# A gated mix of attention and GLU on one core: first key weights in pieces, x turned in four parts, one load moved, all work in a new order

## The chip, the core and the metric

The kernel runs on one core of a Trainium2 chip. The core has a matrix engine (TensorE, PE in the profile), a vector engine (DVE), an engine for activations (ACT), a general one (POOL) and one that only issues DMAs (SP). Each runs its own instructions in order; semaphores connect them. The metric is the device time of one execution in microseconds (us), the median of several runs.

## What is computed

x is 2048 tokens by 512. Two branches read it, and a sigmoid of x·gate_w mixes them per token. Branch A is attention with 32 heads of 16, in 4 segments of 512 tokens, with a memory M, z carried from one segment to the next. Branch B is a gated linear unit of inner width 1792. All weights are bfloat16.

```python
for s in range(N):                       # N = 4 segments of L = 512 tokens
    logits = einsum('bhqd,bhkd->bhqk', qs, ks) * scale + mask
    a_dot = einsum('bhqk,bhkd->bhqd', softmax(logits), vs)
    pq = phi(qs)                         # phi(t) = t+1 if t>0 else exp(t)
    a_mem = einsum('bhld,bhde->bhle', pq, M) / (einsum('bhld,bhd->bhl', pq, z)[..., None] + 1e-06)
    outs.append(g * a_mem + (1.0 - g) * a_dot)
    M = M + einsum('bhld,bhle->bhde', phi(ks), vs);  z = z + phi(ks).sum(over l)
a = concat(outs) @ wo
b = (gelu(x @ w_gate) * (x @ w_up)) @ w_down
return gate * a + (1 - gate) * b         # gate = sigmoid((x * gate_w).sum(-1))
```

## The kernel before

The program is a list of tasks. A task is a few instructions on one engine, or on one of two (an eviction of a PSUM bank can go to ACT or to DVE). `dense` makes a group of four products of 512 columns into one of four PSUM banks. For segment s the groups are K{s}_{t}, Q{s}_{t} (t = 0 to 3), G{s}_{ft} (gate) and U{s}_{ft} (up), ft = 0 to 13, all at L448; V{s}_{m}a and b are half groups of 256 and 257 columns (L498), where column 257 gives the token gate. `Kev`, `Qev`, `Vev`, `Gev` are their evictions, `gd` and `gelu` the activations of the gate, `h` the product of gate and up, `out` the down product (L734), `wo` the output product (L748), `wev` and `oev` their evictions, `dma` the stores. Attention: `st{s}_{t}{A..E}` fills all of the scores' buffer psX (L601), `exp` takes it through the exponential to one of ten buffers (ACT, L608), `msk` masks it (POOL, L614), `pv` multiplies with V (L643), two head groups at a time. Then `tp`, `pvp`, `ota`, `otm` (DVE) bring it to the output's layout. Memory: `phk`, `phq` (a, b, c) compute phi, `ktr` and `otr` are DMA transposes, `mz` the memory's update (L576), `nd` and `ndp` its reading (L546). `vsh` copies V to a second layout by DMA.

The order of all tasks is written out by hand, as one long string `ORDER`: each word is a task, `:d` or `:a` chooses DVE or ACT, `:2` chooses bank 2. The order among the tasks of one engine is that engine's program; the dependencies are turned into semaphore waits. So any wait of an early task holds everything behind it on its engine, SP's DMA issues too.

The start. x of segment 0 arrives in two ways: tokens 0 to 255 as two plain loads of 128 KB (x0_0 on SP, x0_1 on ACT, issued at L341 like all plain loads) that PE turns with eight 128-column transposes (`xtr0_p`, L785; `xev0_p`, L794, copies them), and tokens 256 to 511 by two DMA transposes (x0_t2, x0_t3, L361). wk comes in halves of 256 KB, blocks 2 and 3 on SP and blocks 0 and 1 on ACT. The first key products K0 are cut in parts: a (blocks 2, 3) and b (blocks 0, 1) for tokens 0 to 255, c (all blocks) for the other tokens, 256 columns each (L476), 32 products in all. Before and between, PE runs 52 small products of ones (`warm1`, `warm2`, L382) that nothing reads. Further loads, all on SP in the order of `ORDER`: wq in halves, gate_w (gw), beta (to all 128 partitions), wv, the gate weights wg0, the four transposes of x of segment 1 (x1_0 to x1_3, L345), the up weights wu1, and later wg1, wd0, wd1, wu0, wo and x2. wv waits for x0_t3, wg0 for wq1, x1 for wq0, wu1 for wg0, x2 for wu1, wo for wu0.

Of the kernel before, what the change touches and what calls it, by code (L numbers as in the profile page):

```python
# [248 lines left out]
def _build(es, nc, A_x, A_wq, A_wk, A_wv, A_wo, A_beta, B_w_gate, B_w_up, B_w_down, gate_w, out):  # L249
# [131 lines left out]
    for name, n, cols in (("warm1", 45, 80), ("warm2", 7, 80)):  # L381
        one(name, PE, 3.0, [I(lambda e, cols=cols: e.matmul(BK[s0.i][:, 0:cols], ones, ones[:, 0:cols], start=True, stop=True),  # L382
                              [], [bk(s0)]) for _ in range(n)], bias=9000.0, opens=name == "warm1")
# [400 lines left out]
    for p in (1, 0):  # L784
        one(f"xtr0_{p}", PE, 4 * T_TR, [I(lambda e, q=q, kb=kb, p=p: e.transpose(  # L785
            XB[:, 1024 * p + (kb % 2) * 256 + q * 128:1024 * p + (kb % 2) * 256 + q * 128 + 128],
            pt[stage[0]][:, q, kb * 128:(kb + 1) * 128], ident[:, :]),
            [("xs", 0, 0), ("xs", 0, 1), ("pt", stage[0]), ("ident",)], [("X", p)]) for kb in (2 * p, 2 * p + 1) for q in (0, 1)])
# [79 lines left out]
Qev0_2:d phka0_0 V1_2b:1 V0_0a:3 G1_6:2 V1_0b:0 Vev1_2b:d phka0_2 st0_0E Vev0_0a:d Vev1_0b:d G0_1:1 bexp Gev1_6:a  # L868
exp0_0E Gev0_1:d Q1_2:3 V1_3b:2 V1_3a:0 kpada0_3 Qev1_2:d Vev1_3a:d phkb0_2 phkc0_2 Vev1_3b:d st0_1A gz0 gqa exp0_1A
gr0 Q1_0:1 V1_0a:3 G1_5:0 Vev1_0a:d gqb Gev1_5:d st0_1B Q1_1:2 K1_0:3 exp0_1B phkb0_0 ld_wu1 ld_x2_0 G0_5:0 Qev1_0:d  # L870
kpadb0_3 vsh0_21 st0_1C exp0_1C Qev1_1:d ld_x2_1 ld_x2_3 ktr0_3 ld_wg1 Gev0_5:d V1_2a:1 K1_3:2 K1_1:0 vsh0_01
Vev1_2a:a vsh0_20 ld_x2_2 ktr0_2 vsh0_00 ld_wd1 st0_1D phkc0_0 Kev1_1:d kpada1_1 G0_4:1 G0_3:0 Gev0_4:d Kev1_0:d
Gev0_3:d Kev1_3:a ld_wd0 ld_wu0 ktr0_1 ktr0_0 vsh1_20 ld_wo V1_1a:2 Vev1_1a:d exp0_1D st0_2A exp0_2A msk0_0B msk0_0D
msk0_0C kpada1_0 msk0_0E goa0 gob0 msk0_0A msk0_1A msk0_1C msk0_1D gfull msk0_1B G0_0:1 Q1_3:3 G1_1:0 Qev1_3:d phqa1_0
st0_2B Gev0_0:d Gev1_1:a pv0_1:2301 exp0_2B tp0_d01 tp0_d00 pvp0_01 Q2_0:3 Qev2_0:d tp0_d11 st0_2C K1_2:2 Kev1_2:d
pvp0_00 tp0_d10 gelu0 G0_8:3 G0_13:1 gd0_13 G0_10:2 G0_11:0 G0_9:1 gd0_8 gd0_10 gd0_9 gd0_11 G0_12:3 G0_7:2 gd0_12
G1_2:1 U0_0:0 gd0_7 Gev1_2:d pvp0_11 h0_0 U0_13:3 U0_10:2 h0_10 Q2_1:1 Qev2_1:d exp0_2C st0_2D mz0:0 U0_7:2 U0_9:1
pvp0_10 h0_13 exp0_2D phqb1_0 st0_2E exp0_2E phka1_0 h0_7 mza0 h0_9 ota0_0 phqa1_2 kpadb1_0 G1_4:3 U0_1:2 h0_1
Gev1_4:a V1_1b:0 st0_3A G1_0:1 U0_5:3 Q2_2:2 exp0_3A Vev1_1b:a Gev1_0:a Qev2_2:a kpadb1_1 st0_3B exp0_3B U0_11:0
U0_4:1 U0_12:2 st0_3C phkb1_0 exp0_3C phqc1_0 kpada1_2 h0_4 h0_5 U0_6:1 U0_2:3 h0_11 h0_12 phqb1_2 h0_2 G1_3:0  # L880
Gev1_3:d h0_6 kpadb1_2 st0_3D phka1_2 U0_3:2 h0_3 U0_8:3 h0_8 Q2_3:0 Qev2_3:d exp0_3D phkb1_2 msk0_2A msk0_2B msk0_2C
msk0_3A msk0_2E msk0_2D msk0_3C goc0 msk0_3B st1_0A msk0_3D pv0_3:1230 exp1_0A st1_0B exp1_0B tp0_d20 tp0_d21 pvp0_20
tp0_d30 ota0_1 pvp0_21 tp0_d31 kpada1_3 out0_1_0:1 out0_1_1 out0_1_2 V2_0a:2 Vev2_0a:d G1_9:3 V2_1b:0 Vev2_1b:d
wev0_1:d st1_0C G1_8:2 G1_10:0 G1_11:1 gelu1 gd1_9 G1_7:3 gd1_8 gd1_10 gd1_7 gd1_11 G1_13:2 gd1_13 G1_12:0 gd1_12
phqc1_2 phkc1_0 mzq0 pvp0_31 pvp0_30 ota0_3 V2_0b:3 Vev2_0b:d ota0_2 V2_1a:1 Vev2_1a:d out0_0_0:2 out0_0_1 out0_0_2
nd1_0:0 ndp1_0 phkc1_2 exp1_0C st1_0D exp1_0D K2_0:3 K2_2:1 wev0_0:d Kev2_0:d Kev2_2:a K2_1:0 st1_0E Kev2_1:d U1_2:2
h1_2 wo0_1:1 nd1_3:3 nd1_1:0 exp1_0E st1_1A ld_x3_2 vsh1_00 vsh2_01 ktr1_1 ktr1_0 oev0_1 ndp1_1 wo0_0:2 oev0_0
kpada2_0 vsh1_21 out0_2_0:1 nd1_2:0 msk1_0C msk1_0A exp1_1A st1_1B exp1_1B msk1_0B gz1 msk1_0E msk1_1A msk1_0D msk1_1B
out0_2_1 wo0_2:2 ndp1_2 st1_1C exp1_1C nd1_5:0 out0_2_2 ndp1_3 wev0_2:a ndp1_5 out0_3_0:3 st1_1D nd1_4:0 out0_3_1
out0_3_2 ktr1_2 dma0 vsh1_01 otr1_3 ndp1_4 otr1_0 oev0_2 phka2_0 msk1_1C wev0_3:d ktr1_3 dma1 vsh2_00 otr1_1 ld_x3_1  # L890
ld_x3_0 ld_x3_3 exp1_1D st1_2A exp1_2A gr1 msk1_1D pv1_1:1023 st1_2B exp1_2B tp1_d01 tp1_d00 kpadb1_3 V2_2b:0
Vev2_2b:d K2_3:1 Kev2_3:a G2_3:0 pvp1_00 Gev2_3:d tp1_d10 st1_2C U1_8:1 G2_1:0 otr1_2 V2_3a:2 h1_8 Gev2_1:d Vev2_3a:d
kpadb2_0 kpadb2_1 exp1_2C st1_2D phkb2_0 exp1_2D G2_6:1 wo0_3:0 U1_3:2 pvp1_01 tp1_d11 Gev2_6:a h1_3 phka2_2 oev0_3
st1_2E U1_0:3 V2_3b:1 G2_0:2 Gev2_0:d h1_0 Vev2_3b:d exp1_2E phkb2_2 st1_3A mz1:0 G2_4:2 G2_5:3 pvp1_10 mza1 Gev2_5:d
exp1_3A st1_3B exp1_3B Gev2_4:d U1_11:1 G2_2:0 Gev2_2:d ota1_0 U1_13:3 h1_13 U1_10:2 h1_10 h1_11 G2_11:0 G2_10:3
pvp1_11 phkc2_0 phkc2_2 ota1_1 otm1_0 otm1_1 G2_12:2 G2_9:1 st1_3C gelu2 gd2_11 gd2_12 G2_7:0 G2_13:2 gd2_10 gd2_9
gd2_7 gd2_13 G2_8:3 gd2_8 U1_7:1 U2_9:0 K3_0:2 h1_7 U2_5:3 Q3_0:1 phqa2_0 h2_9 h2_5 Qev3_0:d Kev3_0:d exp1_3C st1_3D
exp1_3D U1_1:0 U2_12:3 msk1_3A msk1_2A msk1_3B U2_13:1 h2_12 h1_1 h2_13 kpada2_1 st2_0A U1_9:2 V2_2a:3 U2_7:0 msk1_2D
msk1_2B msk1_2E h1_9 Vev2_2a:d vsh2_20 dma2 dma3 ktr2_0 ktr2_2 vsh2_21 exp2_0A phqb2_0 msk1_3D msk1_2C msk1_3C st2_0B
h2_7 kpada2_2 pv1_3:1230 tp1_d21 exp2_0B tp1_d20 V3_1a:2 Vev3_1a:a st2_0C exp2_0C pvp1_21 tp1_d31 U1_6:1 Q3_1:2  # L900
V3_0a:0 st2_0D h1_6 pvp1_20 Vev3_0a:d Qev3_1:a V3_2b:1 U1_4:2 U1_5:0 exp2_0D st2_0E exp2_0E tp1_d30 phqc2_0 h1_5 h1_4
ota1_2 Vev3_2b:a U1_12:3 h1_12 pvp1_31 pvp1_30 out1_1_0:0 st2_1A V3_1b:2 out1_1_1 V3_3a:3 exp2_1A st2_1B msk2_0B
msk2_0D Vev3_3a:a exp2_1B out1_1_2 U2_4:1 msk2_0E goa1 gob1 kpadb2_3 kpada2_3 msk2_0C msk2_0A msk2_1A ota1_3 h2_4
otm1_2 otm1_3 K3_1:3 mzq1 Vev3_1b:a wev1_1:a st2_1C msk2_1B goc1 U2_1:2 Q3_3:1 V3_0b:0 Kev3_1:d kpada3_0 h2_1 Qev3_3:d
kpadb2_2 exp2_1C msk2_1C st2_1D V3_2a:3 U2_6:2 exp2_1D Vev3_2a:a wo1_1:1 Vev3_0b:d kpadb3_0 h2_6 oev1_1 st2_2A msk2_1D
pv2_1:0231 exp2_2A st2_2B exp2_2B tp2_d00 pvp2_00 phqa2_2 tp2_d01 tp2_d10 pvp2_10 pvp2_01 tp2_d11 out1_0_0:0 out1_0_1
# [52 lines left out]
```

## Time and profile before

| | us |
|---|---|
| median of three runs | 263.89 |
| the runs | 263.14, 263.89, 518.72 |
| the profiled execution | 264.53 |
| its span, first to last instruction of the program | 262.8 |

The span is what the profile's page and the trace's views show; times in them are from its start. A row of the page's groups, for example, reads: line, engine, operation, what is written and read with shapes, count, then busy time, mean length of one, and the engine's idle time before them:

```
L608 ACT ACTIVATE pt<-psX 128x2048 bf16<-128x2048 f32 x72 | 135.1, 1877 | 29.5 <-PE psX L601 27.9
L614 POOL TENSOR_TENSOR pt<-pt,ctri 128x256 bf16<-128x256 bf16 x128 | 92.6, 734 | 128.3 <-ACT pt L608 123.8
L448 PE MATMUL psD<-xT,wu 128*128 128x512 bf16 x224 | 54.6, 380 | 0.0
L448 PE MATMUL psD<-xT,wg 128*128 128x512 bf16 x224 | 53.4, 380 | 1.1 <-DMA wg<-in_B_w_gate_dram 1.1
```

Matrix products are pipelined: one of 512 columns is 380 ns long, but the next starts 216 ns after it. The distance from start to start is what counts for PE's time. In the same execution 15.68 MB went over SP's DMA queue and 0.39 MB over ACT's.

### The profile page before, as it was taken

The numbers are of one execution on the slowest core, as the hardware profiler recorded it, in microseconds if no ns is written. First come the engines' busy times: TensorE is split into PE (matmuls) and PEld (weight loads), VectorE is DVE, ScalarE is ACT, GpSimd is POOL, SyncE is SP. The second block draws the span as 40 slices with busy tenths as digits, with TensorE's granted clock in tenths as the row PEclk, the third lists the DMA queues.
The fourth block names the chain that finished last, engine by engine and source line by source line (L and its number), as shares of the span: only waits on it lengthen the run. The fifth ranks groups of instructions, "written<-read, shape, count | busy, mean of one in ns | idle before, by whom it ended". The sixth has DMA issues, their size and how long they took to land.

```text
span 262.8 us, 6704 instructions
## 1 busy us (share of the span) xinstructions
PE 257.9 (98%) x2849; PEld 122.5 (47%) x2849; DVE 197.4 (75%) x412; ACT 203.2 (77%) x171; POOL 99.1 (38%) x163
## 2 busy tenths in 40 slices
PE   8989999999999999999999999999999999999995
PEld 8645445444454444544445445444444434444542
DVE  1658878284888686778968988976895973899873
ACT  1569879889998878898988898788788788777312
POOL 5006672024500465104806284156500477345300
PEclk9999999999999999999999999999999999999999
DMA  7795699300010211430003100022430000001432
GB/s 186 244 160 144 163 278 275 93 2 1 5 28 2 61 43 39 91 75 2 2 0 71 35 0 2 2 41 61 68 79 0 2 1 22 3 0 42 62 42 80
DMA packets 31974, 16.50 MB, mean 63 GB/s; under 512 B 21576, under 2 KB 31944, under 8 KB 31944
## 3 DMA queue, kind: packets, MB, share of 16 engines
q1 hardware_dynamic: 31528, 15.68, 27.2%
q8 instruction: 22, 0.36, 0.6%
q10 hardware_dynamic: 416, 0.39, 0.4%
q14 instruction: 8, 0.07, 0.1%
HBM read 7.87 MB, written 2.10 MB: 38 GB/s over the span
## 4 chain that ended last, share of the span: by engine, by line
PE 92%; DMA 4%; SPq 1%; issue 0%; DVE 0%; DVEq 0%
PE psD L448 47%; PE psD L734 19%; PE psX L601 9%; PE psD L643 6%; PE psD L748 5%; PE psD L498 5%; DMA wg<-in_B_w_gate_dram 3%; PE psD L546 1%; DMA wq<-in_A_wq_dram 1%; SPq L361 1%; PE psD L576 1%; SPq L341 1%; DVE ost L752 0%; DVEq L817 0%
## 5 line engine op out<-in xcount | busy, mean ns | idle before, releaser
L608 ACT ACTIVATE pt<-psX 128x2048 bf16<-128x2048 f32 x72 | 135.1, 1877 | 29.5 <-PE psX L601 27.9
L614 POOL TENSOR_TENSOR pt<-pt,ctri 128x256 bf16<-128x256 bf16 x128 | 92.6, 734 | 128.3 <-ACT pt L608 123.8
L448 PE MATMUL psD<-xT,wu 128*128 128x512 bf16 x224 | 54.6, 380 | 0.0
L448 PE MATMUL psD<-xT,wg 128*128 128x512 bf16 x224 | 53.4, 380 | 1.1 <-DMA wg<-in_B_w_gate_dram 1.1
L734 PE MATMUL psD<-wd,gb 128*128 128x512 bf16 x224 | 53.2, 380 | 0.0
L719 DVE TENSOR_TENSOR gb<-psD,gb 128x512 bf16<-128x512 f32 x56 | 37.2, 681 | 10.8 <-PE psD L448 10.7
L448 PEld LDWEIGHTS psD<-xT,wg 128*128 128x128 bf16 x224 | 20.8, 98 | 25.8 <-issue 2.6
L734 PEld LDWEIGHTS psD<-wd,gb 128*128 128x128 bf16 x224 | 20.7, 98 | 24.3 <-issue 2.1
L448 PEld LDWEIGHTS psD<-xT,wu 128*128 128x128 bf16 x224 | 20.2, 98 | 24.7 <-issue 2.6
L601 PE MATMUL psX<-qT,kD 32*128 32x192 bf16 (+7 forms) x512 | 28.5, 287 | 0.0
L529 DVE STREAM_TRANSPOSE tT<-psD 128x512 f32<-128x512 f32 x32 | 21.7, 701 | 5.6 <-PE psD L643 5.1
L442 DVE CAST gb<-psD 128x512 bf16<-128x512 f32 x20 | 13.6, 689 | 13.7 <-PE psD L448 13.7
L601 PEld LDWEIGHTS psX<-qT,kD 32*128 32x128 bf16 x512 | 8.2, 92 | 25.1 <-ACT pt L608 13.4
L498 PE MATMUL psD<-wv,xT 128*128 128x257 bf16 (+1 forms) x128 | 18.2, 273 | 0.0
L752 DVE SCALAR_TENSOR_TENSOR ost<-psD,gtok,wds 128x512 bf16<-128x512 f32 (+1 forms) x17 | 11.9, 711 | 7.7 <-PE psD L748 7.6
L667 DVE SCALAR_TENSOR_TENSOR ob<-tT,gq,rc 128x256 bf16<-128x256 f32 x32 | 16.7, 522 | 1.1
L702 ACT ACTIVATE gb<-psD 128x512 bf16<-128x512 f32 x28 | 15.0, 594 | 3.3 <-PE psD L448 3.3
L643 PE MATMUL psD<-pt,vnat 64*17 64x192 bf16 (+7 forms) x512 | 17.1, 283 | 0.0
L643 PE MATMUL psD<-pt,vsh 64*17 64x192 bf16 (+7 forms) x512 | 17.1, 283 | 0.0
L448 PE MATMUL psD<-xT,wq 128*128 128x512 bf16 x64 | 16.3, 379 | 0.0
L748 PE MATMUL psD<-wo,oT 128*128 128x512 bf16 (+1 forms) x68 | 16.2, 367 | 0.0
L498 PEld LDWEIGHTS psD<-wv,xT 128*128 128x128 bf16 x128 | 11.8, 97 | 6.6 <-issue 1.4
(81 smaller groups left out, 257.0 us busy)
## 6 DMA issues: line engine op xcount, KB each, us to landing
out_dram<-ost SPq DMA_DIRECT2D x15, 128.0 KB, 1.8
wg<-in_B_w_gate_dram SPq DMA_DIRECT2D x2, 896.0 KB, 6.5
wu<-in_B_w_up_dram SPq DMA_DIRECT2D x2, 896.0 KB, 8.3
wd<-in_B_w_down_dram SPq DMA_DIRECT2D x2, 896.0 KB, 7.1
vsh<-vnat SPq DMA_DIRECT2D x16, 68.0 KB, 2.9
wq<-in_A_wq_dram SPq DMA_DIRECT2D x2, 256.0 KB, 3.5
...
```

The costliest lines, as they stand in the source:

```text
L448: one(name, PE, n * T_MM, [I(lambda e, i=i: e.matmul(BK[sl.i][:, :], lhs(i), rhs(i), start=(i == 0), stop=(i == n - 1)), reads(i), [bk(sl) ...
L498: one(f"V{s}_{m}{'ab'[hf]}", PE, 2 * T_MM, [I(lambda e, i=i, sl=sl, a=a, z=z, xs=xs: e.matmul(BK[sl.i][:, 0:z - a], xs(i), wv[:, i, a:z], ...
L529: one(f"tp{name}", DVE, 0.605, [I(lambda e, sl=sl, ti=ti: e.transpose(tT[ti][:, :], BK[sl.i][:, :]), [bk(sl)], [("tT", ti)])], bias=bias)
L601: ins.append(I(lambda e, t=t, kb=kb, ncol=ncol, c0=c0, g=g: e.matmul(XALL[:, g * 512 + c0:g * 512 + c0 + ncol], kD[(4 * s + t) % R_KD][32 ...
L608: one(f"exp{s}_{name}", ACT, 2048 * 0.000833 + 0.05, [I(lambda e: e.activation(pt[slot][:, :, :], xin, ACTF.Exp, scale=ATT_SCALE), [("X",) ...
L614: ins.append(I(lambda e, mv=mv: e.tensor_tensor(mv, mv, cm, ALU.mult), [("pt", slot), ("causal",)], [("pt", slot)]))
L643: ins.append(I(lambda e, kb=kb, slot=slot, c0=c0, n=n, g=g, r0=r0, sl=banks[j], va=va: e.matmul(BK[sl.i][32 * g:32 * g + 17, 64 * kb:512], ...
L667: I(lambda e, ti=ti, ri=ri, t=t, j=j, dst=dst: e.scalar_tensor_tensor(out=dst, in0=t_rows(ti), scalar=gq[:, 2 * t + j:2 * t + j + 1], in1= ...
L702: t = one(f"gd{s}_{ft}", ACT, 0.485, [I(lambda e, gi=gi, f=f, sl=sl: e.activation(gb[gi][:, f, :], BK[sl.i][:, :], ACTF.Gelu_apprx_tanh), ...
L719: one(f"h{s}_{ft}", DVE, 0.605, [I(lambda e, sl=sl, gi=gi, f=f: e.tensor_tensor(gb[gi][:, f, :], BK[sl.i][:, :], gb[gi][:, f, :], ALU.mult ...
L734: mm.append(I(lambda e, fb=fb, gi=gi, f=f, q=q, sl=sl: e.matmul(BK[sl.i][:, :], gb[gi][:, f, q], wd[:, fb, :], start=(fb == 0), stop=(fb = ...
L748: one(f"wo{s}_{qt}{sfx}", PE, 4 * T_MM * w / 512, [I(lambda e, kb=kb, q=q, so=so, c=c, w=w: e.matmul(BK[so.i][:, 0:w], oT[:, kb, q], wo[:, ...
```

## The change

1. wk is loaded in three pieces: block 2 on SP (128 KB), block 3 and then blocks 0 and 1 on ACT.
2. The PE transposes of x and their copies are cut in four parts of 256 columns, one for each block, in the order 2, 3, 0, 1, each to its own bank of psX; blocks 2 and 3 are copied by DVE, 0 and 1 by ACT.
3. The warm-up products are 52 of 66 columns in one task ahead of the transposes, instead of 45 and 7 of 80 around them.
4. `ORDER` is new as a whole. At the start: the load of beta stands behind the four transposes of x1; identity on POOL stands behind `masks` and `causal0`; each K0 part c follows its part b earlier; Q0_0 stands ahead of the last eight key products; the first gate product (G0_5 now, G0_6 before) stands behind three Q groups and seven V halves; V products of segment 1 follow soon after. SP's order behind x1 is now beta, vsh0_20, wu1, x2_0, vsh0_01, vsh0_00, wg1, ktr0_0, wd1, vsh0_21, ktr0_1, vsh1_00, x2_1, x2_2, wu0, ktr0_2, ktr0_3, x2_3, wd0, wo. The tasks, their number and their instructions are otherwise the same.

```diff
-    for eng, h in ((SP, 1), (ACT, 0)):
-        ld_w(f"wk{h}", eng, wk[:, halves[h], :], wsrc(A_wk)[:, halves[h], :], [("wk", 2 * h), ("wk", 2 * h + 1)], 0.25)
+    for eng, nm, c in ((SP, "2", slice(2, 3)), (ACT, "3", slice(3, 4)), (ACT, "0", slice(0, 2))):
+        ld_w(f"wk{nm}", eng, wk[:, c, :], wsrc(A_wk)[:, c, :], [("wk", i) for i in range(c.start, c.stop)], 0.125)
...
-    for name, n, cols in (("warm1", 45, 80), ("warm2", 7, 80)):
-        one(name, PE, 3.0, [I(lambda e, cols=cols: e.matmul(BK[s0.i][:, 0:cols], ones, ones[:, 0:cols], start=True, stop=True),
-                              [], [bk(s0)]) for _ in range(n)], bias=9000.0, opens=name == "warm1")
+    one("warm1", PE, 3.0, [I(lambda e: e.matmul(BK[s0.i][:, 0:66], ones, ones[:, 0:66], start=True, stop=True),
+                             [], [bk(s0)]) for _ in range(52)], bias=9000.0, opens=True)
...
-    for p in (1, 0):
-        one(f"xtr0_{p}", PE, 4 * T_TR, [I(lambda e, q=q, kb=kb, p=p: e.transpose(
-            XB[:, 1024 * p + (kb % 2) * 256 + q * 128:1024 * p + (kb % 2) * 256 + q * 128 + 128],
+    for kb in (2, 3, 0, 1):
+        one(f"xtr0_{kb}", PE, 2 * T_TR, [I(lambda e, q=q, kb=kb: e.transpose(
+            XB[:, 1024 * kb + q * 128:1024 * kb + q * 128 + 128],
             pt[stage[0]][:, q, kb * 128:(kb + 1) * 128], ident[:, :]),
...
+        dst, xin, wr = xT[0][:, kb, 0:256], XB[:, 1024 * kb:1024 * kb + 256], [("xT", 0, kb, "h0")]
...
 ORDER = """
-ld_x0_0 ld_wk1 ld_x0_1 warm1:0 ident xtr0_1 xev0_1:d xtr0_0 warm2 xev0_0:d vones0 masks ld_wk0 causal1 gwz ld_x0_t2
-ld_x0_t3 ld_wq0 ld_wq1 ld_gw ld_beta causal0 consts K0_1a:1 K0_3a:2 K0_3b K0_2a:3 K0_0a:0 K0_2b K0_0b K0_1b K0_0c
-K0_2c K0_3c K0_1c Kev0_0:d Kev0_2:d kpadb0_0 kpadb0_2 causal kpada0_0 Kev0_3:a Q0_0:0 Qev0_0:a Q0_1:3 st0_0A gwtr:2
-Kev0_1:d gwev Q0_3:0 ld_wv ld_wg0 Qev0_1:d V0_1b:1 V0_3a:2 V0_3b:3 exp0_0A Qev0_3:d Vev0_3a:a Vev0_1b:a st0_0B
-Vev0_3b:d kpada0_2 kpada0_1 V0_0b:0 V0_1a:2 V0_2a:1 Vev0_0b:d G0_6:3 Gev0_6:d Vev0_1a:d Vev0_2a:d exp0_0B st0_0C
-exp0_0C Q0_2:0 G0_2:3 V0_2b:2 ld_x1_2 ld_x1_1 betab ld_x1_3 ld_x1_0 st0_0D Vev0_2b:a exp0_0D Gev0_2:d kpadb0_1
...
+ld_x0_0 ld_wk2 ld_x0_t2 masks ld_x0_1 ld_wk3 ld_wk0 causal0 vones0 ld_x0_t3 ld_wq0 ld_wq1 gwz ld_gw ident warm1:0
+xtr0_2 xtr0_3 xtr0_0 xtr0_1 xev0_2:d xev0_0:a xev0_1:a xev0_3:d K0_0a:1 K0_2a:2 K0_1a:3 K0_3a:0 K0_1b K0_1c K0_0b
+K0_0c Kev0_1:d K0_2b K0_3b Kev0_0:a kpada0_0 kpadb0_0 ld_wv Q0_0:3 ld_wg0 Qev0_0:a K0_3c gwtr:1 K0_2c ld_x1_0 Kev0_2:d
+kpadb0_2 ld_x1_1 ld_x1_2 st0_0A Q0_3:3 Q0_2:2 Kev0_3:a phka0_0 gwev kpada0_1 Qev0_2:d Qev0_3:d V0_2a:0 exp0_0A st0_0B
+ld_x1_3 V0_3b:1 V0_3a:2 Vev0_3b:d Vev0_2a:a V0_2b:0 consts V0_1b:3 V0_0a:1 exp0_0B st0_0C Vev0_3a:a Vev0_0a:d
+Vev0_2b:d V0_0b:2 Vev0_0b:d kpadb0_1 kpada0_3 G0_5:1 V0_1a:0 Vev0_1a:d phkb0_0 Q0_1:2 exp0_0C st0_0D Qev0_1:d
+Vev0_1b:d Gev0_5:a V1_3a:0 V1_1a:1 Vev1_1a:d V1_0a:2 Q1_2:3 exp0_0D Vev1_0a:a gz0 causal1 causal Qev1_2:d phkc0_0
+phka0_2 st0_0E V1_2b:1 G0_4:2 G0_3:3 Gev0_4:d kpadb0_3 ld_beta Gev0_3:d betab gr0 exp0_0E Vev1_3a:a st0_1A Vev1_2b:a
...
+Gev1_0:d Gev0_2:d msk0_1C msk0_0B msk0_1B msk0_1D vsh0_00 ld_wg1 ktr0_0 ld_wd1 vsh0_21 V1_0b:3 Gev0_1:a st0_2A K1_1:0
+V1_1b:2 G1_6:1 exp0_2A Kev1_1:a Vev1_0b:d Vev1_1b:d Gev1_6:d st0_2B pv0_1:3201 tp0_d00 tp0_d01 ktr0_1 vsh1_00 ld_x2_1
+ld_x2_2 ld_wu0 ktr0_2 ktr0_3 ld_x2_3 ld_wd0 ld_wo K1_2:3 exp0_2B pvp0_00 Kev1_2:d Q1_3:2 st0_2C tp0_d10 Qev1_3:d
+pvp0_01 tp0_d11 gob0 G0_13:3 G0_9:0 G0_10:2 G0_8:1 gelu0 gd0_9 gd0_10 gd0_8 gd0_13 G0_11:0 G0_12:2 gd0_12 gd0_11
+G0_7:1 gd0_7 exp0_2C U0_3:3 pvp0_11 h0_3 U0_6:2 U0_2:0 U0_13:1 h0_13 U0_7:3 h0_7 st0_2D U0_11:1 phqa1_2 h0_6 h0_2
...
+phqc3_2 mza2 pvp3_00 st3_2D U3_11:3 U3_6:0 h3_11 tp3_d10 h3_6 mzq2 exp3_2D st3_2E exp3_2E wo2_0:2 out2_2_0:3 st3_3A
...
 """
```

More of the change, by code (lines that the diff above doesn't have):

```diff
@@ L867 @@
-exp0_0C Q0_2:0 G0_2:3 V0_2b:2 ld_x1_2 ld_x1_1 betab ld_x1_3 ld_x1_0 st0_0D Vev0_2b:a exp0_0D Gev0_2:d kpadb0_1
[L868 to L906, printed above, removed]
@@ L930 @@
+dma14 wo3_3a:3 wev3_3:a oev3_3b dma15b oev3_3a dma15a
 """
```

87 lines of the change are left out of this document (57 added, 30 removed).

## The prediction

> **What bounds the kernel now.** First the busy times and the chain that ended last, from the page; then TensorE's waits.
>
> ```profile
> PE 257.9 (98%) x2849; PEld 122.5 (47%) x2849; DVE 197.4 (75%) x412; ACT 203.2 (77%) x171; POOL 99.1 (38%) x163
> ...
> PE 92%; DMA 4%; SPq 1%; issue 0%; DVE 0%; DVEq 0%
> ```
> ```profile
> PE psD L448 <- DMA wg<-in_B_w_gate_dram: 1.1, 1, 1.1
> ```
>
> TensorE (PE) is the bound, and after the start it waits once in the whole span. So a new order can win nothing in the body: it can only keep it free of waits or add some. Next the chain of waits in order of time (start, length, what), to see where PE takes over and where it lets go.
>
> ```profile
> 4.98 3.47 DMA wq<-in_A_wq_dram
> ...
> 8.47 7.51 DMA wg<-in_B_w_gate_dram
> ...
> 16.12 1.02 PE psD L448 x4
> 17.14 0.33 PE psX L601 x8
> ...
> 19.30 0.44 PE psD L498 x4
> ...
> 43.00 11.33 PE psD L448 x52
> ...
> 258.10 0.88 PE psD L748 x4
> ```
>
> From 16.12 to about 259.0 the chain is PE alone. The rows give its prices: 11.33/52 = 0.218 us for a 512-column product (0.86 to 0.87 for a group of four), 0.44 for half a V group, 0.33 for a score fill plus 0.1 for the switch ahead of it. What can move is the stretch before 16.12 and the 3.8 us after 258.98. The timeline of the start:
>
> ```profile
> 0.82 3.16 PE L382 MATMUL psD<-const-bfloat16-1.0 128*128 128x80 bf16 x45 [0.82 <-PEq L944]
> ...
> 3.78 1.05 PE L785 MATMUL psX<-ident,pt 128*128 128x128 bf16 x8
> ...
> 4.63 0.65 PE L382 MATMUL psD<-const-bfloat16-1.0 128*128 128x80 bf16 x7
> ...
> 5.25 3.65 PE L476 MATMUL psD<-xT,wk 128*128 128x256 bf16 x32
> ```
>
> The first key product starts at 5.25. The landings that the trace's DMA records give: x at 3.43 and 3.60, the halves of wk at 5.12 (SP) and 5.44 (ACT), the two transposed x blocks at 5.98 and 6.45, wq at 7.79 and 8.45, beta 10.12, wv 11.52, wg0 15.98, the four transposes of x1 16.58 to 19.54. Last, the DMA in half microseconds (the last two columns are the DMA share and GB/s):
>
> ```profile
> 7.00:7.50 0.50, 0.50 (x7) 0.46 (x5) 0.00 (x0) 0.00 (x0) 0.00 (x0) 1.00 0.92 319
> 7.50:8.00 0.50, 0.50 (x7) 0.44 (x6) 0.37 (x1) 0.00 (x0) 0.00 (x0) 1.00 0.32 100
> 8.00:8.50 0.50, 0.50 (x7) 0.46 (x5) 0.50 (x2) 0.00 (x0) 0.00 (x0) 1.00 0.20 61
> ```
>
> From 7.5 to 9.0 the DMA moves 61 to 100 GB/s, between stretches of 319 (before) and 309 (after, 9.0 to 9.5). In just that stretch beta's 64-byte packets pass. The hole is 1.5 us x (about 315 - 85)/315 = 1.1 us of transfer, and wv, wg0 and x1 stand behind it.
>
> **Start: warm-ups, x, wk.** The 52 warm-ups shrink from 80 to 66 columns: the 45 took 66.7 ns each at the slow clock (3.0 us from 0.82), 66 columns are 55 ns, so all 52 end near 3.7, about when x can be used (3.60 landed). The seven that filled 4.63 to 5.25 are gone. Identity now stands behind masks and one causal block on POOL: 0.98 + 0.42 + 0.73 us by their rows from 0.78, ready at 2.9, hidden by the load of x; a later x costs nothing, an earlier one up to 0.8. ACT issues a third DMA (0.46 by its row), its table load ends near 3.5 instead of 3.0, and ACT's first copy is due at 4.5: hidden.
>
> x turned: eight transposes at 107 ns as before, 3.70 to 4.55. The two parts that the first keys need come first and are copied by VectorE in halves: 0.425 us for 512 columns by its row, I take 0.27 for 256 (bounds 0.21, half, and 0.42). The second ends at 4.7, against 4.87 now. The key pieces for them, 128 KB on each queue right behind 128 KB of x, land between 3.6 (x) and 5.12 to 5.44 (twice the bytes): I take 4.8, so the first key product starts at 4.85, 0.40 earlier. That gain doesn't last. Eight products (256 columns, 109 ns) end at 5.72; the next needs the rest of wk, now third on ACT's queue. All of it had landed by 6.45 with the same bytes, so its bounds are 5.44 and 6.45; I take 6.0. The one after needs the last transposed block of x: 6.45 at most. With that at 6.48, 14 products more make the first Q group start at 8.01 (8.74 now), but eight key products are left behind it. Its second half starts at 8.01 + 0.43 = 8.44, if wq1 has landed (8.45 now, somewhat earlier without the hole).
>
> **To the first product on x1.** The gate product that waited for wg0 now comes after more Q and V work. From 8.44 the new order has: half a Q group 0.43, eight key products 0.87, the gate transpose 0.04, three Q groups 2.59, eight V halves 3.5, one gate group 0.86, four fills with their switch 1.72: together 10.0, and 0.1 for the fourth fill, which comes just as the third exponential ends. So V of segment 1 can start at 8.44 + 10.1 = 18.55. The old order has the same work from 5.25: keys 3.49, four Q groups 3.46, V 3.5, gate 0.86, fills 1.72, 0.04, that is 13.07, and its one wait, 1.25 between starts: 19.57. The difference is 1.0 us.
>
> Two landings stand in it. wg0 is due at 8.44 + 7.4 = 15.85; 15.98 less 0.2 to 1.1 is in time. x1's last block was at 19.54 and is needed 0.33 after V's start (it is read fourth now): with the whole hole gone V could start at 18.1, with none of it gone at 19.24. I take 0.8 us of the hole, 18.4 to 18.7, hence a gain of **0.85 us**, bounds 0.33 and 1.2. Beta's DMA now costs its hole behind x1, where wu1 stands; wu1's first user is 30 us later.
>
> The Trainium skill ("DMA: Bandwidth & Descriptors", Why small descriptors are slow) counts 3 fixed cycles for a descriptor beside one for every 32 bytes. By it beta's 128 descriptors over 16 engines are some 40 cycles each, next to nothing, and moving beta would win nothing: the gain would be 0.33. The rows above show a hole of 1.1 us, and I go by them.
>
> **Body.** The same groups in another order. I counted PE work between the places that must wait for another engine. Between two fills lies one exponential: 1.877 us by its row, and 2.39 from fill to fill where nothing else is between (216.09 to 218.48 in the chain). The old order has nine pairs of 2.28 to 2.32 by count, the new one seven of 2.28 to 2.29 and one of 2.08 (the fourth and fifth fill of the last segment's third head group): 0.2 us. The heaviest 20 us of PE work hold 23.5 us of ACT work in the new order, at the start, against 21.6; the worst run of ACT work between two fills is over its PE time by 0.6 in the new and 0.8 in the old one, which shows no wait there. Masks come at least 0.35 ahead of their users in both. With 0.1 for the rest I take **+0.3**, bounds 0 and +1.0.
>
> **SP.** The second load of wu (wu0) stands behind a copy of V's second layout for segment 1, which waits for V halves evicted near 37.2; behind that copy wait two transposes of x2, wu0, two key transposes, wd0 and wo. With 0.6 + 1.26 + 1.26 us of issues wu0 goes at 40.5; the first up product on it is at 48.1: 7.6 us. wg1 took 5.46, wu1 behind transposes 5.96: hidden. **End:** last products, evictions and stores as before, after the same last groups: 0, bounds -0.3 and +0.3.
>
> **Sum.** 262.8 - 0.85 + 0.3 = 262.25 us of span. The profiled execution took 264.53 with 262.8 of span; the median shown is 263.89, 0.64 lower. The same -0.55 gives 263.3.
>
> **Rivals.**
> 1. x1's landing takes the place of the wait for wg0: beta wasn't the hole, V starts at 19.24. -0.33 + 0.3 = 0: 263.9. For it: the transposes themselves are slow, 13 to 15 us shows shares over 1 at 93 to 250 GB/s. Against: they start after wg0, which stood behind the hole. 0.20.
> 2. Slower, the clock: products cost 0.83 ns a column until 4.63 and 0.43 from 5.25; full speed came after 4.3 us of unbroken products. Now there is a pause at 4.55 and again at 5.7. If the grant is missed and comes as much later again, at 9.4, only 21 of the 24 key products are done then, Q's second half starts near 10.2 instead of 8.44: +1.75, at 265.1. It decides if a pause of 0.3 us counts. The skill ("TensorE: Matmul & The Clock Gate", Part 1) lets the clock depend on windows of about 3.4 us that run freely; by that the loss would be 1.25, an estimate. The pause of 1.25 at 15 us, which cost no clock here, speaks against it. 0.10.
> 3. Slower, wu0: if it needs the 10.66 us that it takes now (35.11 to 45.77, behind two loads as large), it lands at 51.2 and PE waits 3.1: 266.4. It decides from 7.6 on. Against: wd0 now stands behind it. 0.07.
> 4. A wait of over 5 us that the counts don't show, a queue blocked for long: 0.04.
>
> The forecast has 0.59.
>
> **Range.** Forecast alone 262.4 to 264.9 (from gain 1.2 with body 0 to gain 0.33 with body +1.0, the end ±0.3 on either side). Rivals 1 and 2 reach 265.1; runs differ by 0.75 (263.14 and 263.89). 262.0 to 265.4 leaves out rivals 3 and 4 and what lies below. A change of 2% is 5.3 us, about what a measurement here can tell from none: faster would need more than all that PE waits at the start, 0.01; slower 0.04; within 0.95.
>
> **What would show it.** The first key product near 4.85 with a pause near 5.7; no wait for wg0, at most 0.5 us for x1; the DMA hole gone from 7.5 to 9.0; first V of segment 1 near 18.6; then PE without gaps but one of 0.2 near 231. Wrong, if products after 5.2 cost 0.83 ns a column, if PE waits for wu near 48, or if the chain leaves PE anywhere in the body.

## The result, and the profile after

| | before | after |
|---|---|---|
| median (five runs, six runs) | 264.06 us | 265.75 us |
| lowest to highest | 263.14 to 264.62 | 265.52 to 265.91 |
| profiled execution, its span | 264.53, 262.8 | 265.52, 263.8 |

The ratio is 1.0067 [1.0047, 1.0087]: 1.7 us longer, where 0.6 shorter was forecast; 0.35 above the top of the range. (One run of before, at 518.72, is left out here.) First the busy times and the shares of the chain of waits, from the page of the changed kernel.

```profile
PE 255.0 (97%) x2816; PEld 121.8 (46%) x2849; DVE 195.6 (74%) x404; ACT 206.7 (78%) x181; POOL 95.6 (36%) x163
...
PE 89%; DVE 5%; issue 2%; DMA 1%; SPq 1%; ACT 1%; DVEq 0%
```

The chain now leaves TensorE: 5% of it are VectorE's, where it had none, and 2% are "issue", time in which the engine waited for nothing that the profile shows. (33 product records are missing in this trace, 2,816 of 2,849; that makes most of the 0.2-us "issue" entries below, one per gap, and they are no time. The weight loads, PEld, are complete, and I time by them where a product lacks.) TensorE's waits, in us: total, times, longest:

```profile
PE psD L447 <- issue: 1.3, 8, 0.2
PE psD L381 <- PEq L941: 0.8, 1, 0.8
PE psX L600 <- issue: 0.7, 1, 0.7
PE psD L475 <- DMA xT<-in_A_x_dram: 0.5, 1, 0.5
PE psD L733 <- issue: 0.5, 3, 0.2
PE psD L475 <- DMA wk<-in_A_wk_dram: 0.3, 1, 0.3
```

The wait for the first gate weights (1.1 before) is gone. Two waits of the head are new, 0.3 for the key weights that come third on ScalarE's queue and 0.5 for the last transposed block of x, and one in the body of 0.7 at a fill, line 600. The start, as the chain of waits tells it (start, length, what):

```profile
3.06 3.62 DMA xT<-in_A_x_dram
6.68 0.14 issue
6.82 1.69 PE psD L475 x14
...
16.50 0.05 issue
16.56 0.81 PE psD L447 x3
...
19.00 1.09 PE psD L497 x9
```

The first gate group runs at 16.5 without a wait (the weights landed at 15.46), and V of segment 1 follows its fill at 18.93, against the 19.57 that the prediction counts for the same work in the old order. The DMA in half microseconds, last column GB/s:

```profile
7.50:8.00 0.50, 0.50 (x7) 0.45 (x5) 0.50 (x1) 0.00 (x0) 0.00 (x0) 1.00 0.71 211
8.00:8.50 0.50, 0.50 (x5) 0.38 (x5) 0.14 (x1) 0.40 (x1) 0.00 (x0) 1.00 0.50 136
8.50:9.00 0.50, 0.45 (x3) 0.10 (x2) 0.26 (x1) 0.20 (x1) 0.00 (x0) 1.00 0.72 201
```

The hole of 61 to 100 GB/s has become one of 136 to 211. To see where the win of the head goes, I set the start of the same share of TensorE's work against its price: 0.864 us for four products of 512 columns, 0.439 for a V half, 0.327 for a fill with its switch, 2.08 for an attention pair, summed from the first key product. **Lag** is the start minus that sum, in the profiled runs:

| work done, us | 18 | 54 | 151 | 162 | 187 | 223 | 245 (last product) |
|---|---|---|---|---|---|---|---|
| before | 7.02 | 8.10 | 11.09 | 11.53 | 12.29 | 13.56 | 13.99 |
| after | 6.48 | 7.61 | 10.67 | 11.36 | 12.95 | 14.49 | 14.94 |
| after minus before | -0.54 | -0.49 | -0.42 | -0.17 | +0.66 | +0.93 | +0.95 |

So the head wins half a microsecond and what follows loses 1.5, most of it between 151 and 187 us of work. Three places stand there and ahead of it. The chain near 60 and near 160:

```profile
61.26 1.70 DVE phq L463
62.97 0.34 DVE phk L459
63.30 0.35 DVE vnat L504
63.65 0.04 issue
63.69 0.60 PE psD L447 x2
```
```profile
159.72 0.78 DVE phq L459
160.50 1.11 DVE mzq L583
161.60 0.61 DVE gb L718
162.22 0.05 issue
162.26 0.82 PE psD L747 x3
```

In the first, U0_8 waits 0.21 for a bank whose V half VectorE evicts only behind two pieces of the memory's feature map. In the second, wo1_1 waits 0.32 for a bank that an up product left: its multiplication (gb) stands behind `mzq`, 1.11 us long, whose result the first product reads at 177.03, 15 us later. The third, from the timelines of TensorE and ScalarE:

```profile
190.86 0.28 PE L642 MATMUL psD<-pt,vsh 64*17 64x256 bf16 x4
191.80 0.40 PE L600 MATMUL psX<-qT,kD 32*128 32x448 bf16 x8 [0.67 <-issue]
```
```profile
189.11 1.88 ACT L607 ACTIVATE pt<-psX 128x2048 bf16<-128x2048 f32 x1 [0.17 <-PE psX L600]
```

The exponential that this fill follows ended at 190.99; elsewhere a fill that waits for one starts 0.055 later, here 0.81. No eviction or load that it needs was late. What did come then was a block of TensorE's own program: 22 packets of 16,384 bytes in the span on a queue of instructions, one of them at 189.10, 1.15 us long, just as the attention pair began at 188.99. That pair is 128 loads and 128 products, 256 instructions in 2.08 us. The trace doesn't say whose program the queue carries; the number fits TensorE, whose 5,737 instructions in the trace are 22.4 blocks of 256.

### The profile page after: what moved, and what is told of

The parts are those of the page before. It is cut to its first block, busy times and chain, and to the rows that moved or that the text cites. A ratio compares the mean times of both kernels' runs of the same rounds, so it can differ in the third digit from the quotient of the medians.

```text
span 263.8 us, 6680 instructions
## 1 busy us (share of the span) xinstructions
PE 255.0 (97%) x2816; PEld 121.8 (46%) x2849; DVE 195.6 (74%) x404; ACT 206.7 (78%) x181; POOL 95.6 (36%) x163
## 4 chain that ended last, share of the span: by engine, by line
PE 89%; DVE 5%; issue 2%; DMA 1%; SPq 1%; ACT 1%; DVEq 0%
PE psD L447 43%; PE psD L733 18%; PE psX L600 8%; PE psD L642 6%; PE psD L497 5%; PE psD L747 5%; DVE gb L718 1%; DMA xT<-in_A_x_dram 1%; PE psD L545 1%; PE psD L475 1%; ACT pt L607 1%; PE psD L575 1%; DVE phq L463 1%; SPq L361 0%; DVE oT L673 0%
## 5 line engine op out<-in xcount | busy, mean ns | idle before, releaser
L613 POOL TENSOR_TENSOR pt<-pt,ctri 128x256 bf16<-128x256 bf16 x128 | 88.3, 701 | 134.4 <-ACT pt L607 130.0
L718 DVE TENSOR_TENSOR gb<-psD,gb 128x512 bf16<-128x512 f32 x56 | 37.3, 682 | 22.4 <-PE psD L447 22.3
L447 PE MATMUL psD<-xT,wu 128*128 128x512 bf16 x214 | 52.7, 380 | 1.2 <-issue 1.0
L733 PE MATMUL psD<-wd,gb 128*128 128x512 bf16 x216 | 51.8, 380 | 0.8 <-issue 0.5
L447 PE MATMUL psD<-xT,wg 128*128 128x512 bf16 x217 | 51.3, 379 | 0.5 <-issue 0.2
L497 PE MATMUL psD<-wv,xT 128*128 128x256 bf16 (+1 forms) x128 | 18.2, 273 | 0.0
L738 ACT ACTIVATE wds<-psD,omgt 128x512 f32<-128x512 f32 x9 | 6.0, 687 | 11.9 <-PE psD L733 11.9
```

What stands on the lines that cost most here:

```text
L447: one(name, PE, n * T_MM, [I(lambda e, i=i: e.matmul(BK[sl.i][:, :], lhs(i), rhs(i), start=(i == 0), stop=(i == n - 1)), reads(i), [bk(sl) ...
L497: one(f"V{s}_{m}{'ab'[hf]}", PE, 2 * T_MM, [I(lambda e, i=i, sl=sl, a=a, z=z, xs=xs: e.matmul(BK[sl.i][:, 0:z - a], xs(i), wv[:, i, a:z], ...
L613: ins.append(I(lambda e, mv=mv: e.tensor_tensor(mv, mv, cm, ALU.mult), [("pt", slot), ("causal",)], [("pt", slot)]))
L718: one(f"h{s}_{ft}", DVE, 0.605, [I(lambda e, sl=sl, gi=gi, f=f: e.tensor_tensor(gb[gi][:, f, :], BK[sl.i][:, :], gb[gi][:, f, :], ALU.mult ...
L733: mm.append(I(lambda e, fb=fb, gi=gi, f=f, q=q, sl=sl: e.matmul(BK[sl.i][:, :], gb[gi][:, f, q], wd[:, fb, :], start=(fb == 0), stop=(fb = ...
```

## The experiments

**1. Which half loses.** The order of one kernel was put behind the head of the other: up to the first V group of segment 1 the one, then what is left of the other in its own order. The cut of the first of them:

```diff
 V0_1a:0 Vev0_1a:d phkb0_0 Q0_1:2 exp0_0C st0_0D Qev0_1:d Vev0_1b:d Gev0_5:a
-V1_3a:0 V1_1a:1 Vev1_1a:d V1_0a:2 Q1_2:3 exp0_0D
+causal1 ld_beta causal kpada0_2 G0_6:3 Gev0_6:d G0_2:3 betab exp0_0D Gev0_2:d V1_2b:1
...
```

> The changed kernel's head (wk in pieces, x turned in four parts, beta behind the second x, the new order up to the first V group of the second segment), and from there the order of before. Computes the same. Theory 1 (the head wins about 0.65 us, by the first V group of segment 1 starting at 18.93 against 19.57, and the new order of the body loses about 1.6): about 0.65 below the kernel before, 263.5 with the median of before at 264.16, and no wait of TensorE over 0.3 us after 19. Rival A (the head wins nothing that lasts, for instance because before's wait for the first gate weights is shorter in most runs than the 1.25 of its profiled run): 264.0 to 264.3. Rival B (the head itself costs, through what it moves to later): 265 or more.

> The mirror of the run before: the head of the kernel before, edits and order, up to where the first products on the second x begin, and from there the order of the changed kernel. Computes the same. Theory 1: it has the loss and not the gain, so about 0.65 above the changed kernel, 266.3 to 266.5, with the waits of the changed kernel's trace in place (0.67 after the fourth attention pair, 0.2 to 0.3 near 63 and 162). Rivals A and B (the loss comes from the head or from the seam): 264.2 to 265.

Measured 266.03 and 267.99. Both cuts made waits of their own. For the first, TensorE's waits say:

```profile
PE psD L447 <- DVE gzr L504: 0.9, 1, 0.9
...
PE psD L447 <- DVE betab L762: 0.8, 1, 0.8
```

Two gate groups in one bank stood there behind evictions and behind beta's copy, which waited for its load. So the totals say nothing, rival B included; but past the cut the lags do. From 31 us of work to the end the lag grows by 6.4 in before, 6.5 in the first mixture, 8.0 in after and 8.3 in the second: the loss of about 1.6 goes with the new body, whichever head is ahead of it.

**2. The wait at 191.** The number of warm-up products was changed and nothing else:

```diff
-    one("warm1", PE, 3.0, [I(lambda e: e.matmul(BK[s0.i][:, 0:66], ones, ones[:, 0:66], start=True, stop=True),
-                             [], [bk(s0)]) for _ in range(52)], bias=9000.0, opens=True)
+    one("warm1", PE, 3.0, [I(lambda e: e.matmul(BK[s0.i][:, 0:90], ones, ones[:, 0:90], start=True, stop=True),
+                             [], [bk(s0)]) for _ in range(38)], bias=9000.0, opens=True)
```

The second run has 32 and 107 in these places.

> The changed kernel with 38 warm-up products of 90 columns in place of 52 of 66: the same 3,420 columns, but TensorE's program is 28 instructions shorter ahead of everything else. Theory 2 (the 0.67 us that the second fill of the last segment waits at 191.14 is a wait for TensorE's own instructions: a 16 KB block of them was on its way from 189.10, just as the 256 instructions of the attention products began, which run through in 2.08 us): the end of a block now falls some 28 instructions later, among work that runs longer, so the wait of 0.67 and the 0.16 behind it are gone and the time is 265.0. Rival (the wait is for data, the exponential ahead of it or its operands): the order is the same, so the wait stays at 0.6 to 0.7 and the time at 265.75.

> The same with 32 warm-up products of 107 columns, 40 instructions fewer than the changed kernel. Counted in instructions, the last pair of attention products (near 246) then begins where the pair near 189 began, against the blocks of 256. Theory 2: the wait of 0.67 leaves 191 and comes up anew at the end of that last pair, near 248, at 0.4 to 0.8; the time stays within 0.3 of the changed kernel's. Rival (a wait for data): the wait at 191 stays and none comes near 248. Third way (blocks matter, but only with transposes on the DMA at the same time, as at 189): gone at 191, none near 248, 265.0.

Measured 265.96 and 266.02. The wait at 191 is gone in both, as theory 2 has it, but the time isn't lower: another came up at a place that I hadn't reckoned with, the attention pair near 71, ahead of which the 64 products of the memory's sums run as quickly. In the run with 38, the weight loads of that pair, and TensorE's waits:

```profile
72.41 0.08 PEld L642 LDWEIGHTS psD<-pt,vnat 64*17 64x17 bf16 x1 [1.03 <-issue]
```
```profile
PE psD L642 <- issue: 0.8, 1, 0.8
```

In the run with 32 there are two, 0.6 near 72 and 0.3 where one was expected, at the end of the last pair, 248.19:

```profile
PE psD L642 <- issue: 0.9, 2, 0.6
```

What settles it: near 72 the two runs halt at different products of the pair, the 60th and the 66th, but at the same one counted from the program's start, the 727th. A wait for data stays with its product; this one stays with the number. The count can be taken further, over all of TensorE's instructions in the traces, the few that handle semaphores too. The five halts of this kind (after, these three and one in the second mixture) come behind 4,289, 1,474, 1,474, 5,569 and 4,290 instructions, and each of these numbers leaves 193 or 194 when divided by 256: every halt is at the same place of a block. The times from the start of the block's packet to the resumption are 2.70 (after), 2.45, 2.25, 2.94, and 2.29 in the second mixture above. When TensorE gets to the end of a block sooner than that, it waits.

**3. The head, mended, and beta alone.** The first mixture with a free bank for the gate group and beta's copy later; the kernel before with beta's load behind x1; the changed kernel with three mends; and the mended mixture with the key products on the first 256 tokens all ahead of the rest.

In this order:

```diff
-G0_6:3 Gev0_6:d G0_2:3 betab exp0_0D
+G0_6:0 Gev0_6:d exp0_0D
...
+exp0_0E Gev0_1:d betab bexp
```
```diff
-ld_gw ld_beta causal0
+ld_gw causal0
...
-ld_x1_2 ld_x1_1 betab ld_x1_3 ld_x1_0
+ld_x1_2 ld_x1_1 ld_x1_3 ld_x1_0 ld_beta
...
-G0_1:1 bexp Gev1_6:a
+G0_1:1 betab bexp Gev1_6:a
```
```diff
+    small = [I(lambda e: e.matmul(BK[s0.i][0:32, 0:16], ones[0:32, 0:32], ones[0:32, 0:16], start=True, stop=True,
+                                  tile_position=(0, 0)), [], [bk(s0)]) for _ in range(32)]
...
-h0_10 msk0_2B gz1 gfull st0_3B gr1 exp0_3B phqc1_2 phka1_2 Vev1_2a:d
+Vev1_2a:d h0_10 msk0_2B gz1 gfull st0_3B gr1 exp0_3B phqc1_2 phka1_2
...
-phqa2_2 mzq1 exp2_1B st2_1C phqb2_0 exp2_1C
+phqa2_2 exp2_1B st2_1C exp2_1C
...
-wo1_1:1 oev1_1 Vev3_3b:a
+wo1_1:1 oev1_1 mzq1 phqb2_0 Vev3_3b:a
```
```diff
-K0_1b K0_1c K0_0b K0_0c Kev0_1:d K0_2b K0_3b
+K0_1b K0_0b K0_2b K0_3b K0_1c K0_0c Kev0_1:d
...
+K0_2c K0_3c Q0_0:3
...
+Q0_3:2 st0_0A Q0_2:3
```

> The new head with the order of before behind it, as in the first run, with its seam mended: the gate group behind the seam goes to a bank that is free, beta's copy on VectorE stands behind four more evictions, and one gate group fills the place that was left empty among the fills of the first segment. Computes the same. Theory 1 (head wins 0.65, new body loses 1.6): no wait of TensorE at the seam, 263.5 to 263.8, that is 0.4 to 0.7 below the kernel before in the same call. Rival A (the win in the head does not last): 264.0 to 264.4, with before's fills waiting for exponentials instead.

> The kernel before with one thing changed: beta's load is issued behind the four transposes of x1, and its copy and exponentials stand accordingly later. Computes the same. Theory 3 (beta's 64-byte packets make the hole of 1.1 us in the DMA): no stretch below 200 GB/s between 7 and 9 us, wv and the first gate weights land 0.5 to 1.1 earlier (gate weights at 14.9 to 15.5 against 15.98), TensorE's wait for them falls from 1.25 to 0.2 to 0.8, and the time by as much: 263.3 to 263.8. Rival (something else makes the hole, the transposes of x or the split of wq for instance): the hole stays, the wait stays at 1.1 to 1.25, and the time is that of before, 264.2.

> The changed kernel with three local repairs: 18 of the 52 warm-up products replaced by 32 very small ones (28 instructions more ahead of all else, so that no block of 256 falls on a pair of attention products or on the sums of the memory write), the eviction of a V group moved ahead of two VectorE pieces of the memory's feature map (near 63), and mzq and an exponential of that map moved behind the output of the second token tile of segment 1 (near 162). Computes the same. Theory 2 and the reading of the waits: the wait of 0.67 with its 0.16, the 0.21 near 63.7 and the 0.32 near 162.3 are gone, no wait for instructions elsewhere, 264.4 to 264.6. Rival (the body's loss is spread over many small delays, and a wait removed comes back at the next fill): 265.2 to 265.75. If blocks hit another place, a wait of 0.4 to 0.8 without a data source stands there.

> The mended new head with the order of before behind it, and besides the key products on the first 256 tokens all ahead of those on tokens 256 to 511, with one more Q group ahead of the first fill and two V halves ahead of the second. Computes the same. Theory 4 (the 0.5 that TensorE waits at 6.82 for the last transposed block of x is a matter of order, and the work drawn ahead is worth it): that wait is gone, the first V group of segment 1 starts 0.4 to 0.5 earlier for the same work, and the time is 263.0 to 263.3. Rival (the exponentials set the pace from the first fill on, near 10.3, so work drawn ahead of it buys nothing): waits for exponentials of 0.3 to 0.6 at the next fills, time as without it, 263.5 to 263.8.

Measured 263.91, 264.94, 265.14 and 264.12, with 264.24 for before: only the first came near what was expected. With beta alone the load did what theory 3 says: the gate weights landed at 15.06 against 15.98, and TensorE waited 0.2 for them. But about two thirds of the hole stayed, counted as what these three stretches lack to 315 GB/s:

```profile
7.50:8.00 0.50, 0.50 (x7) 0.44 (x5) 0.34 (x1) 0.00 (x0) 0.00 (x0) 1.00 0.74 145
8.00:8.50 0.50, 0.50 (x7) 0.45 (x5) 0.50 (x2) 0.00 (x0) 0.00 (x0) 1.00 0.43 80
8.50:9.00 0.50, 0.45 (x5) 0.35 (x5) 0.50 (x2) 0.47 (x1) 0.00 (x0) 1.00 0.80 256
```

and the win was given back where I had put beta's steps. The chain of that run:

```profile
22.44 0.18 DVE betab L763
22.64 0.21 ACT gq L775
22.85 0.12 ACT gfull L776
22.97 0.48 ACT gb L441
23.45 1.77 ACT pt L608
25.22 0.95 ACT phk L462
```

ScalarE stood 1.56 us idle for beta, and the fill near 25 waited 0.7. In the two mixtures TensorE waited 0.2 and 0.6 in the same way, so they don't yet tell the head's worth. In the changed kernel with three mends, the waits at 63.7, 162 and 191 are gone, and two others have come. The first, from the chain:

```profile
41.29 7.23 DMA wu<-in_B_w_up_dram
```

wu's second load took 7.23 from issue to landing where it had taken 6.20, and TensorE waited 0.4 for it. The second was mine: I had taken the exponential of the feature map (phqb2_0) for VectorE's; it is ScalarE's, and moved, it held the next exponential of the scores:

```profile
162.70 0.85 ACT phq L463
...
164.09 1.78 ACT pt L609
165.86 0.05 issue
165.91 0.40 PE psX L602 x8
```

**4. Beta's steps out of the way.** In the two mixtures and in the run with beta alone, the copy, the exponentials and GpSimd's step moved past the second fill of the second head group; in the changed kernel only `mzq` moved, and wu's second load went ahead of two transposes.

```diff
-exp0_0E Gev0_1:d betab bexp
+exp0_0E Gev0_1:d
...
-Gev1_5:d st0_1B Q1_1:2 K1_0:3 exp0_1B
+Gev1_5:d betab st0_1B Q1_1:2 K1_0:3 exp0_1B bexp gqa
```
```diff
-vsh1_00 ld_x2_1 ld_x2_2 ld_wu0
+vsh1_00 ld_wu0 ld_x2_1 ld_x2_2
...
-wo1_1:1 oev1_1 mzq1 phqb2_0 Vev3_3b:a
+wo1_1:1 oev1_1 mzq1 Vev3_3b:a
```

> The run with all key products on the first 256 tokens ahead, and with beta's copy and exponentials moved past the second fill of the second head group, so that ScalarE is not held by a load that lands near 23 to 24. Computes the same. Theory 5 (in the two mended runs and in the one with beta alone, beta's late landing held ScalarE and cost 0.3 to 0.6 at the fill near 25 to 28): no wait over 0.2 there, 263.4 to 263.6, below the kernel before by 0.6 to 0.8. Rival (the wait at that fill is the pace of the exponentials and comes back one fill later): 264.0 to 264.2.

> The kernel before with beta's load behind x1, as in the earlier run, and its copy and exponentials past the second fill of the second head group. Computes the same. Theories 3 and 5 together (the load ahead of wv costs TensorE 0.9 to 1.0 at the gate weights; the place of the exponentials gave it back): the first gate product on wg starts near 15.2 against 16.12, no wait for an exponential near 25, time 263.3 to 263.6. Rival (the fills' exponentials set the pace of the first 40 us, and an earlier gate product is worth nothing): 264.1 to 264.3.

> The changed kernel with the small warm-ups (28 instructions more), the V eviction moved as before, mzq alone moved (the exponential of the feature map is back in its place), and wu's second load ahead of two transposes of x2. Computes the same. Reading of the waits: no wait for instructions, none for wu near 48 (it was 0.4), none at the fill near 165.9 (it was 0.36), 0.2 left near 233: 264.3 to 264.5. Rival (the body's loss comes back elsewhere whatever is mended): 265.0 to 265.2.

> The mended new head with the order of before, and beta's copy and exponentials past the second fill of the second head group: what the head of the change is worth by itself. Computes the same. Theories 1 and 5: 263.5 to 263.7, 0.5 to 0.7 below before. Rival A (the win in the head does not last): 263.9 to 264.2. The run with the key products reordered should be below it by 0.1 to 0.3 if that order helps, level if the exponentials set the pace.

Measured 268.41, 267.93, 264.18 and 267.05 (before 264.01). The changed kernel with four local mends is level with before, and so 1.57 below the changed kernel itself: its wait for x's last block was 0.2, none for instructions or for wu is left, and its lag grows by 6.0 from 54 us of work to the end, where before has 5.9 and after 7.3. The three others lost 2.4 to 3.2 at one place. GpSimd's timeline of the last:

```profile
19.82 0.34 POOL L426 TENSOR_SCALAR gz<-gzr 128x4 f32<-128x4 f32 x1 [14.92 <-DVE ctri L402]
29.73 0.26 POOL L777 TENSOR_SCALAR gq<-gq 128x8 f32<-128x8 f32 x1 [9.57 <-ACT gq L774]
29.94 6.52 POOL L613 TENSOR_TENSOR pt<-pt,ctri 128x256 bf16<-128x256 bf16 x8
```

Its step on beta, 0.26 us long, was first in its queue and held the masks behind it to 29.9; in group 5, where it isn't ahead of them, they begin at 20.41. Eight of them take 6.52, and the first attention pair needs all of the first two head groups'. The medians lost more, 3.0 to 4.4, and in most of these runs the clock fell as well: in the trace with beta alone TensorE's granted clock is 0.5 from 43.40 to 46.81, after a pause of 2.43 that ended at 42.65. Ten of the fourteen runs of these three kernels have a mean granted clock of 0.992 to 0.994, and no other run on record is below 0.998; that the pause brings it about is likely, and not tested.

**5. The head by itself.** The same three with GpSimd's step behind the masks of four fills, and the mended changed kernel with the reordered keys, for which groups among the fills of segment 0 were drawn ahead too (the second diff shows the pair that mattered).

```diff
-exp0_1B bexp gqa
+exp0_1B bexp
...
+msk0_0B msk0_0D msk0_0C kpada1_0 msk0_0E gqa
```
```diff
-st0_2B pv0_1:3201
+K1_2:2 Q1_3:1 exp0_2A Kev1_1:a Kev1_2:d Qev1_3:d st0_2B pv0_1:3201
...
-exp0_2B pvp0_00 Kev1_2:d Q1_3:2 st0_2C
+exp0_2B pvp0_00 st0_2C
```

> As the run with the mended new head and the order of before, but GpSimd's step on beta stands among the masks, behind five of them, and no longer ahead of all. Computes the same. Theory 6 (the last three of these runs lost 2.4 to 3.2 us to GpSimd alone: held by beta until 29.7, its masks came late and the first attention pair waited): that wait is gone and the head's own worth shows, by the state at 37 us of the run before, 0.5 to 0.7: 263.4 to 263.6. Rival (the masks come late in any case or the win is used up by the exponentials): 263.9 to 264.2.

> The same mend for the run with all key products on the first 256 tokens ahead. Computes the same. Theory 6 with theory 4 (that order is worth 0.3 to 0.5 more, by 37.19 against 37.51 at the same work): 263.0 to 263.3. Rival (an earlier start is waited out at the first attention pair, for masks): 263.5 or more.

> The same mend for the kernel before with beta behind x1 and nothing else. Computes the same. Theories 3 and 6: TensorE's wait for the gate weights falls from 1.25 to 0.2 or 0.4, no wait for beta, masks in time, 263.3 to 263.6. Rival (worth nothing): 264.0 to 264.2.

> The changed kernel with its mends (small warm-ups, the V eviction, mzq, wu's second load), and the reordered key products in its head, with five groups drawn ahead among the fills of segment 0. Computes the same. Theory 4: 0.3 to 0.5 below the run with the mends alone, 263.7 to 263.9. Rival (the exponentials set the pace of the first 40 us): 264.1 to 264.3.

Measured 263.90, 263.68, 263.96 and 266.08, before 264.13. The new head with the old body is at 0.9996 [0.9985, 1.0007]: not to be told from before, between rival A and the theory. Beta alone is at 1.0000 [0.9985, 1.0014], though its profiled span of 262.1 shows no wait for the gate weights. With the key products reordered it is 0.9981 [0.9970, 0.9992], 0.45 below before: this version beats both kernels, though 263.0 to 263.3 was expected. Its lag at 18 us of work is 5.9, against 7.0 and 6.5. The old head with beta alone moved has 6.2 to 6.4 there in its three traces, no more than the new head's 6.5: the pieces of wk and the parts of x show no gain of their own at that point. The last run misses: its chain is ScalarE from 40.84 to 47.22, exponential and gelu. A K and a Q group had been drawn from behind the first attention pair to ahead of it; that they had covered ScalarE's work there is likely, and not tested.

**6. The wait for instructions by itself.** The changed kernel with the 32 very small products of the third group in place of 18 warm-ups, and nothing else; and the kernel before with fewer warm-ups, to give it such a wait:

```diff
-for name, n, cols in (("warm1", 45, 80), ("warm2", 7, 80)):
+for name, n, cols in (("warm1", 27, 128), ("warm2", 4, 128)):
```

> The changed kernel with nothing but the small warm-up products: 28 instructions more on TensorE ahead of everything, the order untouched. Computes the same. Theory 2: no wait for instructions anywhere, the wait of 0.67 at 191 and the 0.16 behind it gone, the waits near 63, 162 and 233 still there: 264.9 to 265.0, so half of what the new body loses. Rival (the four mends together did it, this one little): 265.5 or more.

> The kernel before with 31 warm-up products of 128 columns in place of 52 of 80 (27 and 4): 42 instructions fewer ahead of everything, the order untouched. Computes the same. Theory 2, for a kernel that shows no such wait: the last pair of attention products now begins where a block of 256 begins, as in the run with 32 warm-ups, so a wait of 0.5 to 0.7 without a data source comes up at its end near 247, and the time is 0.5 to 0.7 longer, 264.6 to 264.8. Rival (the change's order has to do with it): no wait near 247, time of before, 264.0 to 264.2.

Measured 265.21 (264.37 to 266.71) and 264.40, before 264.25. In the first, no wait for instructions is left: its lag grows by 6.6 from 54 us of work to the end, where after has 7.3 and before 5.9. So this wait is 0.7 of the 1.4 lost there, and 0.7 are waits for data and small delays. The measure is steady over all traces: 5.9 in eleven of the twelve with the old body (6.1 in the run with 31 warm-ups), 7.3 to 7.9 in the four with the new body as it is or with fewer warm-ups, 6.0 in the two with all four mends. The median shows only 0.5 of it, because its runs scatter over 2.3 us; in the profiled one the first gate weights came late:

```profile
PE psD L449 <- DMA wg<-in_B_w_gate_dram: 1.7, 1, 1.7
```

They landed at 17.53 instead of 15.46. The second misses: 0.05 at the end of the last pair, not 0.5. The block's packet started at 244.30, 0.76 ahead of the pair, where in the run with 32 warm-ups it started 0.52 ahead; with 2.25 to 2.94 it is there at 246.6 to 247.2, and the pair ends at 247.14. By the count over all instructions the block ends with the pair, 2.83 after the packet began, so little or no wait was due.

## Why the prediction was wrong

The sum gave 263.34 and the median is 265.75, 2.41 more. By the comparison of the head alone (263.90, before 264.13) 1.55 of this is the body, 0.62 the head, and 0.24 the base: 264.13 for before instead of 263.89.

**First key product, 4.85 with a pause near 5.7.** It began at 4.48 and paused 0.30 until 5.94; the key weights were earlier than taken. The next landing was outside its bound: x's last block "6.45 at most" came at 6.68, its products waited 0.50.

**V of segment 1, 18.55.** 18.93, inside the 18.4 to 19.24 of the parts; no wait for wg0 (15.46) nor for x1 (its blocks at 17.61 to 19.16). Within the profiled pair the term of 0.85 came out at 0.65, inside its bounds. But the gain was read off one execution: spans of before in a later comparison lie between 261.5 and 263.1, median 262.4, and the profiled one is 262.8. Measured by itself, with the old body behind it, the head is worth 0.23 in the median, and no difference that a measurement shows. Why the other executions of before are faster stays open: the two further traces with that head have the same wait of 1.1 for the gate weights.

**The hole.** Beta is part of it: where the old head loads it first, the gate weights land at 15.75 to 15.98 (three traces), where it alone is moved at 14.46 to 15.19 (three). The Trainium skill's price of a descriptor ("DMA: Bandwidth & Descriptors", Why small descriptors are slow), by which the move wins nothing, is not borne out by these landings. But beta is not the whole, as 80 and 145 GB/s remain without it; what makes that rest no run shows.

**Clock.** Key products cost 109 ns each from 4.70 on, ahead of both pauses, and again after them: full speed had come before the first pause, and rival 2 falls. What a pause ahead of it would cost no run shows; the clock fell behind one of 2.4 in the fourth group, and behind these of 0.3 and 0.5 it didn't. Rival 1 falls too: V didn't wait for x1.

**Body, "+0.3, bounds 0 and +1.0".** This step failed. It is 1.5 in the profiled pair and 1.85 between medians (265.75 and 263.90, the new head with either body). Of what was counted, the one wait of 0.2 near 231 is there (0.2 at 233.4). So one of its own signs of being wrong came true: the chain leaves TensorE in the body. The prediction took a count of work between waits for ScalarE and GpSimd as enough. What was not counted: VectorE's queue, which I compared with nothing (0.21 and 0.32, each a bank freed late), and TensorE's own program, which can't be seen in a count of work (0.67 and what hangs on it). Three local changes of order and a shift of 28 instructions take nearly all of it away again (a growth of 6.0 instead of 7.3, before 5.9), which shows that the loss is in these places and not in the order as a whole.

**SP.** wu0 was issued at 41.16 and landed at 47.36, hidden. Its first product ran at 48.29, so the room was 7.1 us and not 7.6. In the mended kernel of the third group it took 7.23 and was late by 0.4: the margin was thinner than a chance of 0.07 for a wait of 3 us suggests. **End:** 0, as forecast.
